# Two small VectorE jobs given to GpSimd in a banded-attention and two-layer MoE kernel, and its instruction order drawn anew

## The chip, the core and the metric

The kernel runs on one core of a Trainium2 chip. Five engines work side by side and wait for each other through semaphores: TensorE (PE: matmuls and transposes, with PEld its weight loads), VectorE (DVE), ScalarE (ACT), GpSimd (POOL) and SyncE (SP), whose queue issues all the DMAs here. The metric is the device time of one execution in microseconds (us). It is compared as the median over several runs.

## The reference, cut to what matters

```python
out_d = softmax(scale * mean4(q) @ mean4(k).T) @ mean4(v)     # "global": groups of 4 positions
out_local = softmax(mask(|i - j| < 4, scale * q @ k.T)) @ v   # "local": a band
x = repeat4(out_d) + out_local                                # 2304 tokens x 512
h = x @ w_in                                                  # 512 -> 1024
ln = layernorm(h * softmax(h)) * g_ln
x = ln @ w_out                                                # 1024 -> 512
h = x @ w2_in                                                 # 512 -> 2048
out = (h * cos(h)) @ w2_out                                   # 2048 -> 512
```

Four batches of 8 heads, 576 positions and 64 columns a head; 2304 tokens in the two layers. The weights and activations come in as float64 words or float32, and the products must be better than one pass of TensorE's reduced float32 gives.

## The kernel before, in words

**Split products.** Every large matmul is made of three (`mm3`, L506 to L509): a number is split into a high part (`hi`, rounded, fp32r) and a low part (`lo` = number minus `hi`), and hi*hi + hi*lo + lo*hi are summed. `split` (L496 to L504) makes `hi` on ScalarE and `lo` on VectorE, by one subtraction with two inputs in SBUF.

**Weights.** `wload` (L528 to L543) loads a block of a weight as 64-bit words and makes float32 of it in three VectorE operations: a shift and mask (L537), an or with the sign (L539), an or with the low word's bits (L541). The first weight, `w1i`, comes in 8 blocks of 512 KB (128 x 512 words); `w1i_step` (L582) loads one and splits it into `w1i_h` and `w1i_l`, two parts of the tile R (in the trace `R<-wu`; in the order's rows `R_75`). `w1o` comes in 8 more.

**Attention.** `Glob.load` (L648) loads the values of one pair of heads as `gv` (72 x 2 x 4 x 128: the four values of a group side by side). `Glob.prep` (L653) sums q and k over groups of four (`pooled`, L661), and the values in two additions: the halves of `gv` (L667, 72 x 512) and then the halves of that into `gvs` (L669, 72 x 256). `Glob.V` multiplies them with the softmax (`gv` in PSUM, L707) into `G`. `Loc.V` makes the local product (`lv`, L770), and one VectorE addition, L772, adds `lv` and `G` into X, the tokens. A 128-token block of X is split (`xsplit`, `P<-X`) and goes into the first layer's matmuls (`h<-R,P`).

**The start.** TensorE has nothing to do until q, k, v and the first weight blocks are there, so 100 matmuls without a use (`idle`, L873) stand in its early gaps. The first `h` needs the first block of X, which needs both pairs of heads of batch 0.

**The order.** `arrange` sorts the instructions of each engine. It replays the whole program with a table of estimated durations (`Step.estimate`), gives each instruction a due time, and shifts the due times of some tiles by a list of seeds, `DRAWS`. The order that comes out is fixed on every engine: an instruction that has to wait holds up what stands behind it on its engine, on SP's queue and on GpSimd too.

Of the kernel before, what the change touches and what calls it, by code (L numbers as in the profile page):

```python
# [9 lines left out]
F32 = mybir.dt.float32  # L10
# [5 lines left out]
ALU = mybir.AluOpType  # L16
# [19 lines left out]
ROUNDS = 20  # L36
SEARCHED = 0.8
DRAWS = (70000001, 70000006, 70000036, 70000042, 70000050, 70000063, 70000081, 70000093, 70000097, 70000106,
# [19 lines left out]

# [73 lines left out]
class Step:  # L132
# [10 lines left out]
    def estimate(self, psum):  # L143
        out, n, kind = self.outs[0], columns(self.outs[0]), self.x.opcode
# [8 lines left out]
        wide = max([n] + [columns(o) for o in self.ins[:1]])  # L153
# [22 lines left out]
        if self.engine == "Pool":  # L176
            return 464 if wide == 1 else 245 + (1.73 if kind == "TensorTensor" else 3.4 if "Ptr" in kind else 0.4) * wide
        return 60.0
# [250 lines left out]
def kernel(  # L429
# [13 lines left out]
    nc = tc.nc  # L443
# [30 lines left out]
    w1i_h = R1[:, 0:W1].rearrange("p (k f) -> p k f", k=KD)  # L474
    w1i_l = R1[:, W1:2 * W1].rearrange("p (k f) -> p k f", k=KD)
# [19 lines left out]

    def split(hi, lo, src, gain=None):  # L496

        if gain is None:
            nc.scalar.activation(out=hi, in_=src, func=AF.Copy)  # L499
            nc.vector.tensor_tensor(out=lo, in0=src, in1=hi.bitcast(F32), op=ALU.subtract)  # L500
        else:
            nc.scalar.activation(out=hi, in_=src, func=AF.Copy, scale=gain)
            nc.vector.scalar_tensor_tensor(out=lo, in0=src, scalar=gain, in1=hi.bitcast(F32),
                                           op0=ALU.mult, op1=ALU.subtract)  # L504
# [22 lines left out]

    def wload(src, place):  # L528

# [4 lines left out]
        low, high = words[:, :, 0], words[:, :, 1]  # L534
        ui = u.bitcast(I32)

        nc.vector.tensor_scalar(out=ui, in0=high, scalar1=3, scalar2=0x3FFFFFFF,  # L537
                                op0=ALU.logical_shift_left, op1=ALU.bitwise_and)
# [43 lines left out]
    def w1i_step(i):  # L582
        k, f = i % KD, slice(i // KD * W1C, (i // KD + 1) * W1C)
        split(w1i_h[:, k, f], w1i_l[:, k, f], wload(w1i[k * 128:(k + 1) * 128, f], stage))

# [39 lines left out]
    class Glob:  # L625
# [27 lines left out]
        def prep(self):  # L653
            if self.a0:
                return
            if self.c % 2 == 0:
                for j in range(2):
# [4 lines left out]
                    if j == 0:  # L662
                        for k in range(2):
                            r = slice(64 * k, 64 * k + 64)
                            nc.scalar.copy(out=pdiag[self.turn][r, :, k], in_=o[r])
            vs = VS[self.b, self.c] = att.tile([SH, 2, 128], F32, tag="gvs", name="gvs", bufs=4)
            nc.vector.tensor_tensor(out=self.v[:, :, 0:2, :], in0=self.v[:, :, 0:2, :], in1=self.v[:, :, 2:4, :],  # L667
                                    op=ALU.add)
            nc.vector.tensor_tensor(out=vs, in0=self.v[:, :, 0, :], in1=self.v[:, :, 1, :], op=ALU.add)  # L669

# [337 lines left out]
    for kk in range(KD):  # L1008
        src = X[:, :TB2, kk, :]
# [237 lines left out]
```

## Time and the profile before

| | before |
|---|---|
| median of 3 runs | 751.3 us (750.54 to 752.64) |
| the profiled execution, its own time | 752.8 us |
| span of its trace, first to last instruction | 751.0 us |
| PE busy | 736.1 us, 98% |
| DVE busy | 607.1 us, 81% |
| ACT busy | 458.3 us, 61% |
| POOL busy | 20.5 us, 3% |
| PE busy with the 100 `idle` matmuls (inside the 736.1) | 17.9 us |

Busy time is the sum of an engine's instruction times within the span. The `idle` matmuls count as busy PE time although they compute nothing that is used. Rows of a timeline give the start, the duration of a merged group, and in brackets how long the engine had been idle before it and what released it.

### The profile page before, as it was taken

Reading aid. Unit: us, or ns where it says so; the run is one execution under the profiler, and the core shown is the slowest. Engines: PE = TensorE matmul, PEld = TensorE weight load, DVE = VectorE, ACT = ScalarE, POOL = GpSimd, SP = SyncE. Lnnn points to the kernel's source line nnn. Section 1 sums busy time; section 2 is a strip of 40 time slices with the busy share of each in tenths; the row PEclk is TensorE's granted clock in tenths of the full one; section 3 lists DMA queues with packets and bytes.
Section 4 is the critical chain, followed back from the end, with each engine's and each line's share of the span. In section 5 each row is a group of like instructions: output and inputs, shape, how many; then the busy total and the mean of one; then the engine's idle time right before and its main releaser. Section 6 shows DMA issues by size and latency. Waiting matters only on the chain.

```text
span 751.0 us, 14309 instructions
## 1 busy us (share of the span) xinstructions
PE 736.1 (98%) x5324; PEld 651.2 (87%) x5324; DVE 607.1 (81%) x1244; ACT 458.3 (61%) x1062; POOL 20.5 (3%) x40
## 2 busy tenths in 40 slices
PE   6899999999999999999999999999999999999998
PEld 5678898898988898889998898899998898898896
DVE  5999999969479799986499996977669676877763
ACT  6477678848465455534577765756556665656654
POOL 3000000000000001000000000000000000000000
PEclk9989999999999999999999999999999999999999
DMA  9956766765265675684354442042212331122201
GB/s 269 278 164 190 214 182 181 192 181 168 69 173 171 213 234 176 206 253 134 99 169 140 127 150 75 29 133 78 79 35 71 113 88 54 29 85 84 60 27 57
DMA packets 76502, 101.92 MB, mean 136 GB/s; under 512 B 23280, under 2 KB 48912, under 8 KB 76432
## 3 DMA queue, kind: packets, MB, share of 16 engines
q1 hardware_dynamic: 76432, 101.00, 44.7%
q8 instruction: 42, 0.69, 0.4%
q14 instruction: 28, 0.23, 0.1%
HBM read 83.67 MB, written 17.30 MB: 134 GB/s over the span
## 4 chain that ended last, share of the span: by engine, by line
PE 73%; DVE 16%; DMA 5%; issue 3%; ACT 2%; SPq 1%; POOL 0%; ACTq 0%; DVEq 0%; POOLq 0%
PE s L507 7%; PE s L508 7%; PE s L509 7%; PE ob L507 4%; PE ob L509 4%; PE ob L508 4%; PE oa L507 4%; PE oa L509 4%; PE oa L508 4%; PE ls L749 3%; PE x L507 3%; PE x L508 3%; PE x L509 3%; PE h L507 3%; PE h L509 3%
## 5 line engine op out<-in xcount | busy, mean ns | idle before, releaser
L508 PE MATMUL x<-P,R 128*128 128x256 f32 x288 | 80.9, 287 | 0.4 <-DVE P L500 0.2
L507 PE MATMUL x<-P,R 128*128 128x256 f32 x288 | 80.5, 288 | 0.3 <-DVE P L500 0.3
L509 PE MATMUL x<-P,R 128*128 128x256 f32 x288 | 80.2, 285 | 0.0
L508 PE MATMUL s<-R 128*128 128x256 f32 x256 | 70.3, 282 | 0.1
L507 PE MATMUL s<-R 128*128 128x256 f32 x256 | 69.9, 283 | 0.5 <-DVE wr L1142 0.2
L509 PE MATMUL s<-R,S_l 128*128 128x256 f32 x256 | 70.1, 282 | 0.0
L507 PE MATMUL h<-R,P 128*128 128x512 f32 x144 | 59.2, 421 | 0.0
L508 PE MATMUL h<-R,P 128*128 128x512 f32 x144 | 57.7, 410 | 0.0
L509 PE MATMUL h<-R,P 128*128 128x512 f32 x144 | 57.4, 409 | 0.0
L508 PEld LDWEIGHTS x<-P,R 128*128 128x128 f32 x288 | 53.5, 188 | 1.9 <-DVE P L500 1.1
L507 PEld LDWEIGHTS x<-P,R 128*128 128x128 f32 x288 | 53.4, 188 | 1.4 <-DVE P L500 0.5
L509 PEld LDWEIGHTS x<-P,R 128*128 128x128 f32 x288 | 53.5, 188 | 0.8 <-issue 0.2
L508 PE MATMUL s<-R,w2i 128*128 128x256 f32 x192 | 52.9, 282 | 0.4 <-DVE R L500 0.4
L507 PE MATMUL s<-R,w2i 128*128 128x256 f32 x192 | 53.0, 281 | 0.0
L509 PE MATMUL s<-R,w2i 128*128 128x256 f32 x192 | 52.7, 281 | 0.0
L609 ACT ACTIVATE le<-ls,sm 128x70 f32<-128x70 f32 x144 | 44.0, 325 | 13.6 <-DVE sm L607 9.7
L1031 ACT ACTIVATE a<-a 128x1024 f32<-128x1024 f32 (+1 forms) x41 | 39.2, 955 | 21.5 <-DVE a L1029 21.1
L499 ACT ACTIVATE GR<-a 128x1024 fp32r<-128x1024 f32 (+1 forms) x41 | 39.3, 958 | 21.0 <-DVE a L1034 20.7
L507 PEld LDWEIGHTS s<-R 128*128 128x128 f32 x256 | 47.4, 188 | 2.1 <-ACT R L499 0.6
L508 PEld LDWEIGHTS s<-R 128*128 128x128 f32 x256 | 47.7, 189 | 1.7 <-DVE R L500 0.7
L509 PEld LDWEIGHTS s<-R,S_l 128*128 128x128 f32 x256 | 47.8, 189 | 0.8
L500 DVE TENSOR_TENSOR GR<-a,GR 128x1024 fp32r<-128x1024 f32 (+1 forms) x41 | 44.7, 1090 | 4.5 <-ACT GR L499 4.2
(171 smaller groups left out, 2167.2 us busy)
## 6 DMA issues: line engine op xcount, KB each, us to landing
wo<-drw SPq DMA_DIRECT2D x80, 256.0 KB
X<-in_w2o_dram SPq DMA_DIRECT2D x32, 256.0 KB
X<-in_w2i_dram SPq DMA_DIRECT2D x32, 256.0 KB
lv<-in_vl_dram SPq DMA_DIRECT2D x48, 105.0 KB
out_dram<-xo SPq DMA_DIRECT2D x18, 256.0 KB
gv<-in_vg_dram SPq DMA_DIRECT2D x16, 256.0 KB
X<-in_w1i_dram SPq DMA_DIRECT2D x8, 512.0 KB
X<-in_w1o_dram SPq DMA_DIRECT2D x8, 512.0 KB
```

Source lines behind the costliest of these rows:

```text
L499: nc.scalar.activation(out=hi, in_=src, func=AF.Copy)
L500: nc.vector.tensor_tensor(out=lo, in0=src, in1=hi.bitcast(F32), op=ALU.subtract)
L507: nc.tensor.matmul(ps, lh, rh, start=start, stop=False)
L508: nc.tensor.matmul(ps, lh, rl, start=False, stop=False)
L509: nc.tensor.matmul(ps, ll, rh, start=False, stop=stop)
L609: nc.scalar.activation(out=e[:, j, :], in_=src[:, j, :], func=AF.Exp, bias=neg[:, j:j + 1], scale=scale, accum_out=ssum[:, j:j + 1])
L749: nc.tensor.matmul(ps[:, i:i + WIN], self.q[:, h, a].rearrange("p j s -> p (j s)"), self.k[:, h, a * QB:a * QB + WIN], start=False, stop=h ...
L1031: nc.scalar.activation(out=a, in_=a, func=AF.Sin, scale=0.5)
```

## The change

`split` and `wload` get an argument `on`, the engine that does one of their operations. `w1i_step` passes GpSimd to `split`: the 8 low parts of the first weight (128 x 512 each) are subtracted by GpSimd. No caller passes `on` to `wload`, so nothing changes there. `Glob.prep` lets GpSimd make both additions of the values for batches 0 and 1, which are 8 pairs of additions (8 of 72 x 512 and 8 of 72 x 256), and leaves batches 2 and 3 on VectorE. The planner's figure for a GpSimd operation with two inputs goes from 1.73 to 2.2 a column. `DRAWS` is another list, of 202 seeds where there were 201, and `SEARCHED` goes from 0.8 to 1, so that shifts can lie anywhere in the program. Line numbers after the list move by 1 or 2.

```diff
-SEARCHED = 0.8
-DRAWS = (70000001, 70000006, 70000036, 70000042, 70000050, 70000063, 70000081, 70000093, 70000097, 70000106,
...
+SEARCHED = 1
+DRAWS = (10000004, 10000024, 10000025, 10000029, 10000044, 10000050, 10000051, 10000058, 10000071, 10000081,
...
-            return 464 if wide == 1 else 245 + (1.73 if kind == "TensorTensor" else 3.4 if "Ptr" in kind else 0.4) * wide
+            return 464 if wide == 1 else 245 + (2.2 if kind == "TensorTensor" else 3.4 if "Ptr" in kind else 0.4) * wide
...
-    def split(hi, lo, src, gain=None):
+    def split(hi, lo, src, gain=None, on=nc.vector):
...
             nc.scalar.activation(out=hi, in_=src, func=AF.Copy)
-            nc.vector.tensor_tensor(out=lo, in0=src, in1=hi.bitcast(F32), op=ALU.subtract)
+            on.tensor_tensor(out=lo, in0=src, in1=hi.bitcast(F32), op=ALU.subtract)
...
-        split(w1i_h[:, k, f], w1i_l[:, k, f], wload(w1i[k * 128:(k + 1) * 128, f], stage))
+        split(w1i_h[:, k, f], w1i_l[:, k, f], wload(w1i[k * 128:(k + 1) * 128, f], stage), on=nc.gpsimd)
...
-            nc.vector.tensor_tensor(out=self.v[:, :, 0:2, :], in0=self.v[:, :, 0:2, :], in1=self.v[:, :, 2:4, :],
+            on = nc.gpsimd if self.b < 2 else nc.vector
+            on.tensor_tensor(out=self.v[:, :, 0:2, :], in0=self.v[:, :, 0:2, :], in1=self.v[:, :, 2:4, :],
                                     op=ALU.add)
-            nc.vector.tensor_tensor(out=vs, in0=self.v[:, :, 0, :], in1=self.v[:, :, 1, :], op=ALU.add)
+            on.tensor_tensor(out=vs, in0=self.v[:, :, 0, :], in1=self.v[:, :, 1, :], op=ALU.add)
```

The order on VectorE, around the addition that completes the first block of X. Before, it stands 72nd, behind the last two value sums (L667, L669) and the fourth low part of the weight (L500):

```order
L661 TENSOR_REDUCE pooled_113<-qt 128x288
L667 TENSOR_TENSOR gv<-gv 72x2x256 x2
L669 TENSOR_TENSOR gvs<-gv 72x256 x2
L500 TENSOR_TENSOR R_75<-wu,R_75 128x512
L537 TENSOR_SCALAR wu<-X 128x512 x2
L539 SCALAR_TENSOR_TENSOR wu<-X,wu 128x512
L772 TENSOR_TENSOR X<-lv,g 128x3x128
L541 SCALAR_TENSOR_TENSOR wu<-X,wu 128x512
```

The same place now; the addition is L774:

```order
L614 TENSOR_TENSOR ge<-ge,sm 96x288
L608 TENSOR_SCALAR sm<-sm 96x2 x2
L662 TENSOR_REDUCE pooled_113<-qt 128x288
L538 TENSOR_SCALAR wu<-X 128x512
L540 SCALAR_TENSOR_TENSOR wu<-X,wu 128x512
L542 SCALAR_TENSOR_TENSOR wu<-X,wu 128x512
L774 TENSOR_TENSOR X<-lv,g 128x3x128
L538 TENSOR_SCALAR wu<-X 128x512
```

Ahead of that addition VectorE has lost 4 additions of 72 x 512, 4 of 72 x 256, 4 subtractions of 128 x 512 and one shift of 128 x 512, and has gained one or (L542) of 128 x 512; every other instruction ahead of it is the same in kind and number, in another order.

GpSimd now has these rows directly behind its memsets and masks at the start. Before, the next row there was the `pow` of the first layer norm (L827):

```order
L669 TENSOR_TENSOR gv<-gv 72x2x256
L671 TENSOR_TENSOR gvs<-gv 72x256
L669 TENSOR_TENSOR gv<-gv 72x2x256
L671 TENSOR_TENSOR gvs<-gv 72x256
L501 TENSOR_TENSOR R_75<-wu,R_75 128x512 x2
L669 TENSOR_TENSOR gv<-gv 72x2x256
L501 TENSOR_TENSOR R_75<-wu,R_75 128x512
L671 TENSOR_TENSOR gvs<-gv 72x256
L501 TENSOR_TENSOR R_75<-wu,R_75 128x512
L669 TENSOR_TENSOR gv<-gv 72x2x256
L671 TENSOR_TENSOR gvs<-gv 72x256
L501 TENSOR_TENSOR R_75<-wu,R_75 128x512 x4
```

The last of the four `gvs` of batch 0, which the first X needs, stands behind four low parts of the weight.

On TensorE, ahead of the first `h` (`h_645` is the bank of the first half). Before, the last `idle` stands in front of 8 `gv`, 12 `lv` and 6 transposes:

```order
L873 MATMUL idle<-mask,identb 128x350
L707 MATMUL gv<-at,gvs 64x48 x8
L770 MATMUL lv<-at,lv 64x64 x12
L689 MATMUL gt<-ident,ge 72x96 x6
L507 MATMUL h_645<-R_75,P 128x512
```

Now those `lv` and half of those `gv` stand earlier, and `idle` matmuls stand behind the last 4 `gv` too:

```order
L709 MATMUL gv<-at,gvs 64x48 x4
L875 LDWEIGHTS identb
L875 MATMUL idle<-mask,identb 128x350
L875 LDWEIGHTS identb
L875 MATMUL idle<-mask,identb 128x350
L875 LDWEIGHTS identb
L875 MATMUL idle<-mask,identb 128x350
L691 MATMUL gt<-ident,ge 72x96 x6
L508 MATMUL h_645<-R_75,P 128x512
L509 MATMUL h_645<-R_75,P 128x512
```

All 100 `idle` still stand ahead of the first `h`. SP's queue has the third and fourth `gv` load (256 and 32 KB each) behind three and four of the `w1i` blocks; before, all four stood ahead of the first block.

## Rows read from the trace of the kernel before

**Rows 1.** The page, part 1: busy time, share of the span, instructions.
```profile
span 751.0 us, 14309 instructions
PE 736.1 (98%) x5324; PEld 651.2 (87%) x5324; DVE 607.1 (81%) x1244; ACT 458.3 (61%) x1062; POOL 20.5 (3%) x40
```

**Rows 2.** Stretch; busy us (instructions) of PE, PEld, DVE, ACT, POOL; clock, DMA share, GB/s.
```profile
0.00:40.00 40.00, 31.27 (x260) 23.33 (x261) 31.45 (x80) 22.22 (x79) 6.88 (x22) 0.97 0.89 263
...
60.00:140.00 80.00, 79.81 (x704) 69.01 (x702) 79.97 (x204) 60.57 (x220) 3.33 (x5) 1.00 0.66 188
140.00:350.00 210.00, 208.68 (x1724) 187.87 (x1724) 176.31 (x501) 119.12 (x372) 10.31 (x13) 1.00 0.60 182
350.00:740.00 390.00, 389.05 (x2459) 349.24 (x2459) 299.99 (x414) 239.06 (x326) 0.00 (x0) 1.00 0.28 85
```

**Rows 3.** Timeline of TensorE up to the first `h`.
```profile
29.78 4.17 PE L873 MATMUL idle<-mask,identb 128*128 128x350 bf16 x27
35.72 0.68 PE L707 MATMUL gv<-at,gvs 72*64 72x48 f32 x16 [1.77 <-DVE gvs L669]
...
38.31 0.85 PE L689 MATMUL gt<-ident,ge 96*72 96x96 f32 x4 [0.90 <-DVE X L772]
38.97 0.80 PE L507 MATMUL h<-R,P 128*128 128x512 f32 x1
```

**Rows 4.** Timeline of VectorE: its first instruction, and the same stretch.
```profile
6.44 1.35 DVE L661 TENSOR_REDUCE pooled<-qt 128x288 f32<-128x1152 f32 x1 [6.44 <-DMA qt<-in_q_dram]
...
33.96 1.28 DVE L667 TENSOR_TENSOR gv<-gv 72x512 f32<-72x512 f32 x2
35.16 0.75 DVE L669 TENSOR_TENSOR gvs<-gv 72x256 f32<-72x256 f32 x2
35.83 0.68 DVE L500 TENSOR_TENSOR R<-wu,R 128x512 fp32r<-128x512 f32 x1
36.43 0.75 DVE L537 TENSOR_SCALAR wu<-X 128x512 int32<-128x512 int32 x2
37.10 0.68 DVE L539 SCALAR_TENSOR_TENSOR wu<-X,wu 128x512 int32<-128x512 int32 x1
37.71 0.55 DVE L772 TENSOR_TENSOR X<-lv,g 128x384 f32<-128x384 f32 x1
38.17 0.68 DVE L541 SCALAR_TENSOR_TENSOR wu<-X,wu 128x512 int32<-128x512 int32 x1
38.77 1.34 DVE L661 TENSOR_REDUCE pooled<-kt 128x288 f32<-128x1152 f32 x1
```

**Rows 5.** Groups of GpSimd by shape: columns as in part 5 of a page.
```profile
L827 POOL TENSOR_TENSOR st<-st,nhalf 128x1 f32<-128x1 f32 x18 | 13.6, 758 | 322.3 <-DVE st L825 303.4 <-DVE R L500 18.8
L868 POOL TENSOR_SCALAR_AFFINE_SELECT mask<-mask 64x350 bf16<-64x350 bf16 x4 | 2.0, 498 | 0.2
...
L868 POOL TENSOR_SCALAR_AFFINE_SELECT mask<-mask 64x70 bf16<-64x70 bf16 x4 | 1.0, 240 | 0.1
```

**Rows 6.** Instructions of two lines: duration ns min/median/max, first and last start.
```profile
L827 POOL TENSOR_TENSOR st<-st,nhalf x18: 548/604/1341, 71.3 to 343.3; 128x1 f32<-128x1 f32 x18
...
L500 DVE TENSOR_TENSOR w2i<-X,w2i x16: 413/416/422, 268.0 to 312.4; 128x256 fp32r<-128x256 f32 x16
```

**Rows 7.** Timelines of GpSimd and VectorE around one `pow`.
```profile
268.27 1.14 POOL L827 TENSOR_TENSOR st<-st,nhalf 128x1 f32<-128x1 f32 x1 [1.27 <-DVE st L825]
...
268.05 0.42 DVE L500 TENSOR_TENSOR w2i<-X,w2i 128x256 fp32r<-128x256 f32 x1
268.38 0.42 DVE L539 SCALAR_TENSOR_TENSOR X<-X 128x256 int32<-128x256 int32 x1
```

**Rows 8.** The chain that ended last, about 9 us: start, length, what.
```profile
9.06 3.77 DMA lv<-in_vl_dram
```

**Rows 9.** Busy time by stretch, columns as in group 2.
```profile
35.00:40.00 5.00, 3.38 (x50) 2.81 (x51) 5.00 (x10) 2.27 (x7) 0.00 (x0) 0.76 0.74 202
40.00:45.00 5.00, 5.00 (x21) 4.14 (x21) 4.35 (x11) 2.85 (x12) 0.00 (x0) 0.56 0.52 156
```

More of the change, by code (lines that the diff above doesn't have):

```diff
@@ L494 @@
     xh1, xl1 = [part((2 * KF + i * KD) * GT, 2, KD, 128) for i in range(2)]
-    def split(hi, lo, src, gain=None):
+    def split(hi, lo, src, gain=None, on=nc.vector):
         if gain is None:
             nc.scalar.activation(out=hi, in_=src, func=AF.Copy)
-            nc.vector.tensor_tensor(out=lo, in0=src, in1=hi.bitcast(F32), op=ALU.subtract)
+            on.tensor_tensor(out=lo, in0=src, in1=hi.bitcast(F32), op=ALU.subtract)
         else:
             nc.scalar.activation(out=hi, in_=src, func=AF.Copy, scale=gain)
-            nc.vector.scalar_tensor_tensor(out=lo, in0=src, scalar=gain, in1=hi.bitcast(F32),
+            on.scalar_tensor_tensor(out=lo, in0=src, scalar=gain, in1=hi.bitcast(F32),
                                            op0=ALU.mult, op1=ALU.subtract)
@@ L525, in bank, with wload @@
         return psum.tile([128, 512], F32, tag=tag, name=name, bufs=bufs)
-    def wload(src, place):
+    def wload(src, place, on=nc.vector):
         n = src.shape[1]
@@ L535, in wload @@
         ui = u.bitcast(I32)
-        nc.vector.tensor_scalar(out=ui, in0=high, scalar1=3, scalar2=0x3FFFFFFF,
+        on.tensor_scalar(out=ui, in0=high, scalar1=3, scalar2=0x3FFFFFFF,
                                 op0=ALU.logical_shift_left, op1=ALU.bitwise_and)
```

39 rows, old and new, of the table DRAWS are left out of this document.

## The prediction

> **What bounds the kernel now.** I read the page first: PE is busy for 736.1 of 751.0 us, with POOL almost unused [rows 1]. A share over the whole run hides where the rest lies, so the second view is busy time by stretch. From 60 to 140 us PE is busy for 79.81 of 80, from 140 to 350 for 208.68 of 210, from 350 to 740 for 389.05 of 390 [rows 2]: over 680 us it lacks 0.19 + 1.32 + 0.95 = 2.46 us. There TensorE is the bound. VectorE is busy too, 79.97 of 80 us between 60 and 140, but TensorE does not wait for it, so time taken off VectorE there buys at most those tenths. What can be won lies in the first 40 us: PE is busy for 31.27 of them, and 17.9 us of that are the useless `idle` matmuls (the table above). Afterwards the useful matmuls run as a queue that is always full, so the end of the run moves by as much as its start moves.
>
> The third view is TensorE's timeline up to that start. The `idle` run out at 33.95, PE waits 1.77 us for the value sum L669 and 0.90 us for the addition L772, and the first `h` starts at 38.97 [rows 3]. The fourth is VectorE's timeline in the same stretch: its instructions stand back to back, two L667, two L669, a low part L500, then L772 at 37.71 [rows 4]; ScalarE makes the high part behind it, and `h` follows. So the first `h` comes when VectorE has worked through what stands ahead of L772.
>
> **What is taken from VectorE ahead of L772.** I use the distance from one start to the next, since neighbours overlap by some 0.08 us [rows 4]: L667 twice takes 35.16 - 33.96 = 1.20, so 0.60; L669 twice 35.83 - 35.16 = 0.67, so 0.335; L500 36.43 - 35.83 = 0.60; L537 twice 37.10 - 36.43 = 0.67, so 0.335; L541 38.77 - 38.17 = 0.60. The order takes away 4 L667, 4 L669, 4 L500 and one L537 and puts in one L541: 2.40 + 1.34 + 2.40 + 0.335 - 0.60 = 5.9 us. All other rows ahead of it are the same, so without a new wait the first `h` starts at 38.97 - 5.9 = 33.1. The other operations that leave VectorE (4 low parts, 4 pairs of sums of batch 1) stand behind the first `h`, where TensorE is the bound; I cost them at nothing. Their cover is the queue of ready matmuls in 60 to 140 us, where VectorE would even have to fall back to cost anything.
>
> **What GpSimd gets.** Ahead of that X it has 12 operations in a row: 4 sums of 72 x 512, 4 of 72 x 256 and 4 low parts of 128 x 512. The trace shows none of this kind. The nearest rows have one input: 0.240 us for 70 columns, 0.498 for 350 [rows 5], so 0.92 ns a column, and 512 columns at least 0.65 us. If each of two inputs costs that much, 512 columns take 0.24 + 2 x 0.92 x 442 = 1.05 us and 256 columns 0.58 us, an estimate; I take it, as the only price that counts both inputs. The 12 are then 8 x 1.05 + 4 x 0.58 = 10.7 us (6.8 by one input: 8 x 0.65 and 4 x 0.41). The Trainium skill (GPSIMD Engine Reference, Performance versus the Vector engine) gives 4497 ns for a two-input addition of 2048 columns, 1.12 us for 512; by that the 12 would be about 11.2 us. No run here shows it yet.
>
> When can they start? The queue issues a `lv` load at 9.06, just behind the four `gv` loads, and it lands 3.77 us later [rows 8], so the `gv` are there by about 12.8. The third and fourth `gv` now stand behind up to four blocks of 512 KB: 4 x 0.524 MB at 263 GB/s [rows 2] are 8 us, so the fourth lands near 21, and its two sums end near 23; the 12 in a row, from 12.8 on, near 23.5. The last `gvs` is needed 3.1 us ahead of the first `h` (35.91 against 38.97 now [rows 3, 4]), so by 30.0 where `h` comes at 33.1. GpSimd has over 6 us in hand there, and its slower arithmetic costs nothing by itself.
>
> **What the two engines do to each other.** This is the unknown. The 18 `pow` of 128 x 1 take 548 ns at least but 1341 at most [rows 6] and 758 on the mean [rows 5]. At 268.27 one takes 1.14 us while VectorE runs an L500 and an L539 one behind the other [rows 7]: GpSimd is held up by VectorE. The other way nothing is seen: that L500 keeps to 0.42 us, and the 16 of its shape lie between 413 and 422 ns [rows 6]. But a `pow` reads one column, and the new operations read 512. Bounds: VectorE loses nothing, or it stands still for all 10.7 us. I take the mean hold-up of the `pow`, 758 - 548 = 0.21 us, for each of the 12: 2.5 us. It is near the lower bound because the nearest rows show no stretched VectorE instruction at all.
>
> The Trainium skill (SBUF — State Buffer, Who interferes with whom) speaks against the change: a VectorE instruction with two SBUF inputs and a GpSimd one that reads SBUF exclude each other, and the later one waits for the whole of the earlier. The stretched `pow` agrees with one half of that; the other half is not in this trace. By this rule the sum would be that of the second rival below.
>
> **The sum.** The first `h` moves by 5.9 - 2.5 = 3.4 us, to 35.6. The profiled execution would take 752.8 - 3.4 = 749.4 us; it lay 1.5 above the median of the runs, so the median goes from 751.3 to **747.9 us**. A difference under 0.3% (2.25 us) is about what a measurement of this kernel cannot tell from none.
>
> **The rest of the new order** moves thousands of rows. The instructions on TensorE are the same in number, and of the stretches behind 60 us only 2.46 us can be won; a new order can lose that much as easily. I cost it at nothing, with about 1.5 us either way.
>
> **Rivals.**
>
> *The clock stays up.* Behind the gaps at 34 to 38 us the granted clock is 0.76 of 2.4 GHz in 35 to 40 and 0.56 in 40 to 45 [rows 9], which is time at the 1.2 GHz level; it costs 5 x 0.24 + 5 x 0.44 = 3.4 us of full-speed work. In the new order three `idle` stand between the last `gv` and the transposes ahead of `h`, so the gaps may be filled. If the clock does not fall: 747.9 - 3.4 = 744.5. Against it: a GpSimd that is late opens the same gaps.
>
> *VectorE is held.* A GpSimd operation that has begun holds any VectorE instruction with two SBUF inputs. VectorE's list ahead of L774 takes 37.71 - 6.44 - 5.9 = 25.4 us [rows 4], and over 6 us of it are such instructions (10 ors of 0.60, and 8 smaller products of the softmax). If half of GpSimd's 10.7 us falls on them, VectorE loses 5.4, and 0.5 of the 5.9 is left: 750.8. For it: the hold-up is seen in one direction. Against it: most of the list can run meanwhile.
>
> *GpSimd is late (slower).* Its 12 operations stand in one queue, and the first X waits for the last of them. They end near 23.5 without waits and cost nothing until 35.9, so this decides from (35.9 - 23.5)/12 = 1.0 us of waiting per operation. At 1.5 us each, about twice the longest wait of a `pow` (0.79), the last `gvs` comes at 41.5, 5.6 us later than now: 756.9. VectorE's back-to-back ors are what could starve it.
>
> *The move does nothing*, because the loads set the pace: the DMA share is 0.89 over the first 40 us [rows 2]. Then 751.3. VectorE is busy in all of 35 to 40 [rows 9], which speaks against it.
>
> **Chances.** My forecast (746 to 750) 0.40; the clock stays up (744.5) 0.19; VectorE held (750.8) 0.23; GpSimd late (756.9) 0.13; nothing 0.05. Of the forecast's 0.40 a small part lies above 749.05, and some of "held" lies below it: faster by over 0.3% 0.60, within 0.3% 0.26, slower 0.14. The range for 8 in 10 reaches from 743.0, under the clock's case, to 753.0, over that of a held VectorE and short of a late GpSimd.
>
> **What would show it.** The first `h` near 35.6 us and not 38.97; 12 GpSimd operations ahead of the last `gvs`, of about 1.05 and 0.58 us plus waits; VectorE's two-input instructions (0.68 us for 512 columns) no longer than now; PE with no more than 3 us of gaps behind 60 us. It is wrong if those VectorE instructions stretch to a microsecond or more beside GpSimd, if PE waits for POOL ahead of the first `gv`, or if the first `h` moves and the end does not.

## The result, and the profile after

| | before | changed |
|---|---|---|
| median | 752.0 us (750.5 to 752.7, 4 runs) | 762.0 us (760.9 to 763.6, 4 runs) |
| ratio, with its 95% interval | 1 | 1.0138 (1.0113 to 1.0162) |
| profiled execution, its span | 752.8, 751.0 us | 763.6, 761.5 us |
| first `h` | 38.97 us | 42.83 us |

The change makes the kernel slower, by 10 us. The page of the changed kernel, part 1, against [rows 1]:

```profile
span 761.5 us, 14324 instructions
...
PE 741.1 (97%) x5324; PEld 652.8 (86%) x5324; DVE 607.1 (80%) x1220; ACT 457.3 (60%) x1062; POOL 55.9 (7%) x64
```

VectorE has lost 24 instructions and is busy for exactly as long as before, 607.1 us. So those that are left have become longer by as much as was saved. The timeline of VectorE in the changed kernel, ahead of the addition L774 that completes the first X (start, length, and in brackets an idle time):

```profile
12.68 0.31 DVE L612 TENSOR_SCALAR sm<-sm 128x6 f32<-128x6 f32 x1 [1.97 <-ACT le L610]
...
13.25 1.55 DVE L614 TENSOR_TENSOR le<-le,sm 128x420 f32<-128x420 f32 x1
...
24.85 1.64 DVE L542 SCALAR_TENSOR_TENSOR wu<-X,wu 128x512 int32<-128x512 int32 x1
...
28.05 1.16 DVE L608 TENSOR_SCALAR sm<-sm 96x2 f32<-96x2 f32 x1
29.14 0.68 DVE L542 SCALAR_TENSOR_TENSOR wu<-X,wu 128x512 int32<-128x512 int32 x1
...
30.16 2.16 DVE L614 TENSOR_TENSOR ge<-ge,sm 96x144 f32<-96x144 f32 x1
...
36.12 1.31 DVE L608 TENSOR_SCALAR sm<-sm 96x2 f32<-96x2 f32 x2
37.35 1.34 DVE L662 TENSOR_REDUCE pooled<-qt 128x288 f32<-128x1152 f32 x1
...
39.14 1.10 DVE L540 SCALAR_TENSOR_TENSOR wu<-X,wu 128x512 int32<-128x512 int32 x1
40.28 0.69 DVE L542 SCALAR_TENSOR_TENSOR wu<-X,wu 128x512 int32<-128x512 int32 x1
40.89 0.55 DVE L774 TENSOR_TENSOR X<-lv,g 128x384 f32<-128x384 f32 x1
```

The L542 at 24.85 takes 1.64 us, the one at 29.14 takes 0.68, as its kind did before [rows 4]. Seven rows ahead of L774 are more than 0.2 us longer than their kind in the trace of before, by 6.8 us together. And here is GpSimd in the same stretch:

```profile
10.90 1.26 POOL L669 TENSOR_TENSOR gv<-gv 72x512 f32<-72x512 f32 x1 [2.76 <-DMA gv<-in_vg_dram]
12.24 0.72 POOL L671 TENSOR_TENSOR gvs<-gv 72x256 f32<-72x256 f32 x1
...
24.20 1.74 POOL L501 TENSOR_TENSOR R<-wu,R 128x512 fp32r<-128x512 f32 x1 [8.82 <-ACT R L500]
27.23 1.97 POOL L501 TENSOR_TENSOR R<-wu,R 128x512 fp32r<-128x512 f32 x1 [1.29 <-ACT R L500]
29.16 1.78 POOL L669 TENSOR_TENSOR gv<-gv 72x512 f32<-72x512 f32 x1
30.90 1.26 POOL L501 TENSOR_TENSOR R<-wu,R 128x512 fp32r<-128x512 f32 x1
...
36.14 1.27 POOL L501 TENSOR_TENSOR R<-wu,R 128x512 fp32r<-128x512 f32 x1 [2.89 <-ACT R L500]
37.37 1.45 POOL L669 TENSOR_TENSOR gv<-gv 72x512 f32<-72x512 f32 x1
38.90 0.80 POOL L671 TENSOR_TENSOR gvs<-gv 72x256 f32<-72x256 f32 x1
```

Lay the two views on each other: each stretched VectorE row begins while a GpSimd operation runs, or within 0.02 us of its start, and ends with it or within 0.6 us behind it, as if it had waited and then run. The longest, at 30.16, outlasts two operations, the L669 of 29.16 and the L501 of 30.90. The L542 of 24.85 ends at 26.49, 0.55 behind the L501 of 24.20 to 25.94; the L608 at 28.05, of two columns, ends at 29.21 with the L501 that ends at 29.20. The reduction at 37.35 runs beside an L669 and keeps its 1.34 us. GpSimd in turn waits three times for ScalarE's high parts (L500), which wait for VectorE's ors, so its last sum of batch 0 ends at 39.70 and not near 23.5.

X needs that sum as well as VectorE. Behind the sum come the last 8 `gv` on TensorE and `g` on ScalarE:

```profile
38.50 1.66 PE L875 MATMUL idle<-mask,identb 128*128 128x350 bf16 x10
40.09 0.44 PE L709 MATMUL gv<-at,gvs 72*64 72x48 f32 x8
```

```profile
35.44 0.63 ACT L500 ACTIVATE R<-wu 128x512 fp32r<-128x512 f32 x1 [1.09 <-DVE wu L542]
40.57 0.25 ACT L712 ACTIVATE g<-gv 128x96 f32<-128x96 f32 x1 [0.98 <-PE gv L709]
```

`g` is ready at 40.82, just as VectorE comes to the end of its L542 and X starts at 40.89. Both paths end together, and both go back to the stretched rows: GpSimd's low part at 36.14 waits for ScalarE's R of 35.44, which waits for a VectorE or that ends at 35.40, and 5.3 of the 6.8 us of stretch lie ahead of that.

Behind the first `h`, the row of TensorE's timeline with its longest wait there, and the windows around it against [rows 2, 9] (busy us of PE, PEld, DVE, ACT, POOL; clock, DMA share, GB/s):

```profile
60.78 0.85 PE L761 MATMUL lt<-ident,le 128*70 128x128 f32 x3 [1.79 <-DVE X L774]
```

```profile
55.00:60.00 5.00, 3.99 (x41) 2.89 (x41) 5.00 (x7) 3.75 (x14) 4.84 (x5) 1.00 0.97 334
60.00:65.00 5.00, 4.22 (x36) 3.30 (x37) 4.69 (x14) 2.44 (x7) 0.92 (x1) 0.57 0.32 107
65.00:70.00 5.00, 5.00 (x25) 4.81 (x25) 3.25 (x11) 2.78 (x13) 0.00 (x0) 0.50 0.16 37
70.00:75.00 5.00, 5.00 (x20) 4.14 (x20) 3.87 (x8) 3.73 (x12) 0.00 (x0) 0.57 0.47 143
```

From 55 to 60 us VectorE is busy all the time with 7 instructions, GpSimd with 5; TensorE runs dry and waits for the next X, and behind that gap the granted clock is at the 1.2 GHz level for most of 60 to 75. That costs 5 x (0.43 + 0.50 + 0.43) = 6.8 us of full-speed work, against 3.4 before [rows 9]. In this one execution the 10.5 us between the spans are thus: 3.9 from the later first `h`; 4.0 more in gaps of TensorE behind it (10.2 against 6.2 us); and 2.6 by which TensorE's busy time behind the first `h` is longer (708.5 against 705.9 us for the same work), which is the longer matmuls of the low clock (less than the 3.4 between the two sums above, since part of the low clock falls on gaps, and in before a part lies ahead of `h`). Of the 4.0 us of gaps 2.3 lie ahead of 80 us and 1.8 behind it. From 140 to 350 us, for instance, TensorE is now busy for 207.18 us, where it was 208.68 [rows 2]:

```profile
140.00:350.00 210.00, 207.18 (x1701) 184.54 (x1700) 179.92 (x514) 120.63 (x389) 14.50 (x13) 1.00 0.62 188
```

### The profile page after: what moved, and what is told of

Its sections match the earlier page's. It is cut to its first block, busy times and chain, and to the rows that moved or that the text cites. A ratio compares the mean times of both kernels' runs of the same rounds, so it can differ in the third digit from the quotient of the medians.

```text
span 761.5 us, 14324 instructions
## 1 busy us (share of the span) xinstructions
PE 741.1 (97%) x5324; PEld 652.8 (86%) x5324; DVE 607.1 (80%) x1220; ACT 457.3 (60%) x1062; POOL 55.9 (7%) x64
## 4 chain that ended last, share of the span: by engine, by line
PE 71%; DVE 19%; ACT 4%; issue 3%; DMA 3%; POOL 1%; DVEq 0%; POOLq 0%; ACTq 0%; SPq 0%
PE s L508 6%; PE s L509 6%; PE s L510 6%; PE ob L510 4%; PE oa L508 4%; PE oa L510 4%; PE oa L509 4%; PE ob L508 4%; PE ob L509 4%; PE ls L751 3%; PE x L509 3%; PE x L508 3%; PE x L510 3%; PE h L508 2%; PE h L510 2%
## 5 line engine op out<-in xcount | busy, mean ns | idle before, releaser
L509 PE MATMUL x<-P,R 128*128 128x256 f32 x288 | 78.7, 287 | 2.0 <-DVE P L501 2.0
L508 PE MATMUL x<-P,R 128*128 128x256 f32 x288 | 78.4, 287 | 0.0
L510 PE MATMUL x<-P,R 128*128 128x256 f32 x288 | 77.9, 284 | 0.0
L508 PE MATMUL h<-R,P 128*128 128x512 f32 x144 | 60.5, 425 | 0.7 <-ACT P L500 0.7
L509 PE MATMUL h<-R,P 128*128 128x512 f32 x144 | 59.0, 415 | 0.0
L510 PE MATMUL h<-R,P 128*128 128x512 f32 x144 | 57.8, 409 | 0.3 <-DVE P L501 0.3
L509 PEld LDWEIGHTS x<-P,R 128*128 128x128 f32 x288 | 52.6, 188 | 3.2 <-DVE P L501 2.9
L500 ACT ACTIVATE GR<-a 128x1024 fp32r<-128x1024 f32 (+1 forms) x41 | 39.2, 958 | 25.8 <-DVE a L1036 22.3
L508 PEld LDWEIGHTS x<-P,R 128*128 128x128 f32 x288 | 52.5, 188 | 0.8 <-ACT P L500 0.4
L510 PEld LDWEIGHTS x<-P,R 128*128 128x128 f32 x288 | 52.6, 188 | 0.1
L500 ACT ACTIVATE w2i<-wo 128x512 fp32r<-128x512 f32 x58 | 36.0, 624 | 24.8 <-PE ob L510 14.3
```

The costliest lines, as they stand in the source:

```text
L508: nc.tensor.matmul(ps, lh, rh, start=start, stop=False)
L509: nc.tensor.matmul(ps, lh, rl, start=False, stop=False)
L510: nc.tensor.matmul(ps, ll, rh, start=False, stop=stop)
```

## The experiments

Three theories. **HOLD**: a GpSimd operation that reads SBUF stops VectorE's instructions. **LATE**: GpSimd is slower and waits for ScalarE, and TensorE waits for its results. **ORDER**: the new order is a worse one, whoever makes the sums. The times of all kernels, with the first `h` and the stretch (how much longer VectorE's rows ahead of the first X are than in before, rows by more than 0.2 us) of the profiled execution, and TensorE's gaps in it (its idle time from 80 to 740 us):

| kernel | median us | ratio to before, 95% | first `h` | stretch | gaps |
|---|---|---|---|---|---|
| before | 752.0 | 1 | 38.97 | 0 | 2.45 |
| changed | 762.0 | 1.0138 (1.0113 to 1.0162) | 42.83 | 6.8 | 4.25 |
| x1 new order, sums on VectorE | 756.2 | 1.0059 (1.0039 to 1.0079) | 39.99 | 0 | 4.82 |
| x2 old order, sums on GpSimd | 756.0 | 1.0050 (1.0031 to 1.0068) | 41.99 | 6.4 | 2.30 |
| x3 old order, weight only | 755.1 | 1.0044 (1.0025 to 1.0063) | 41.69 | 2.6 | 2.11 |
| x4 old order, values only | 753.2 | 1.0031 (1.0019 to 1.0044) | 40.78 | 4.3 | 1.92 |
| x6 old order, first pair only | 751.7 | 1.0010 (0.9997 to 1.0023) | 39.27 | 1.1 | 2.47 |
| x7 changed, memsets | 750.6 | 0.9993 (0.9980 to 1.0006) | 40.32 | 2 (below) | 4.03 |
| x8 changed, copies | 751.7 | 1.0009 (0.9994 to 1.0023) | 38.60 | 1.6 | 5.39 |
| x11 changed, two copies each | 756.5 | 1.0069 (1.0053 to 1.0085) | 39.93 | 2.6 | 6.31 |
| x9 before, no seeds | 758.9 | 1.0106 (1.0091 to 1.0121) | 39.05 | 0 | 5.93 |
| x10 changed, no seeds | 770.2 | 1.0258 (1.0218 to 1.0297) | 42.17 | 6.3 | 3.61 |

The five kernels with the new order (changed, x1, x7, x8, x11) have 4.0 to 6.3 us of gaps, the five with the order of before 1.9 to 2.5, whichever engine makes the sums (one trace of each). That is a cost of the new order of its own, 1.5 us or more.

### The two engines by themselves (m1_port)

```diff
+    for i in range(16):
+        V.tensor_tensor(out=c, in0=a, in1=b_, op=ALU.add)
+        if i < 10:
+            G.tensor_tensor(out=f, in0=d, in1=e, op=ALU.add)
...
```

> This kernel leaves the whole computation out and times the two engines against each other, stage by stage: VectorE alone, GpSimd alone, and both, with five kinds of VectorE instruction beside GpSimd additions of 128 x 512, and one stage with GpSimd memsets. Theory HOLD (a GpSimd operation that reads SBUF holds VectorE instructions with two SBUF inputs or in the two-column mode): beside GpSimd additions of about 1.27 us, VectorE additions of 512 columns go from 0.68 us alone to 1.5 us or more where one falls behind a GpSimd operation, and so do tensor_scalar instructions, even of 6 columns; reductions and additions with one input in PSUM keep their 0.6 to 0.7 us; beside memsets the additions keep 0.68 us. Theory ORDER or LATE (VectorE is not held, the time is lost by the new order or by waiting for GpSimd): VectorE durations are the same in all stages within 5%.

Its groups by shape (count | busy us, mean ns); the alone case of each engine comes first, then VectorE beside GpSimd's additions (beside its memsets in L478):

```profile
L467 DVE TENSOR_TENSOR vc<-va,vb 128x512 f32<-128x512 f32 x16 | 11.1, 693 | 0.9 <-ACT vb L461 0.4
L470 POOL TENSOR_TENSOR gc<-ga,gb 128x512 f32<-128x512 f32 x10 | 12.6, 1262 | 17.8 <-ACT vb L461 17.1
L473 DVE TENSOR_TENSOR vc<-va,vb 128x512 f32<-128x512 f32 x16 | 20.5, 1280 | 15.4 <-ACT vb L461 14.9
...
L478 DVE TENSOR_TENSOR vc<-va,vb 128x512 f32<-128x512 f32 x16 | 11.1, 692 | 1.5 <-ACT vb L461 0.9
L483 DVE TENSOR_REDUCE vc<-va 128x1 f32<-128x512 f32 x16 | 11.0, 686 | 1.3 <-ACT va L459 0.8
L488 DVE TENSOR_TENSOR vc<-pp,va 128x512 f32<-128x512 f32 x16 | 11.1, 691 | 3.1 <-ACT va L459 2.6
L493 DVE TENSOR_SCALAR vc<-va 128x512 f32<-128x512 f32 x16 | 16.2, 1015 | 3.1 <-ACT va L459 2.5
L498 DVE TENSOR_SCALAR vc<-va 128x6 f32<-128x6 f32 x32 | 15.0, 467 | 1.8 <-ACT va L459 0.8
L503 DVE TENSOR_TENSOR vc<-va,vb 128x512 f32<-128x512 f32 x12 | 10.5, 879 | 1.3 <-ACT vb L461 0.9
```

An addition of 512 columns takes GpSimd 1.26 us. Beside it (L473) VectorE's additions take 1280 ns instead of 693: 16 x 0.587 / 10 = 0.94 us lost for each GpSimd operation. Beside GpSimd's memsets (L478) the additions lose nothing. As reductions (L483) or with one input in PSUM (L488) VectorE's instructions take 686 and 691 ns; no run has them alone, but GpSimd's additions beside them keep their 1.26 us too, so neither engine seems to lose. Where every other VectorE instruction is a reduction (L503) VectorE's loss is 12 x 0.186 / 10 = 0.22 us, and there GpSimd's additions take 1.60 us instead of 1.26. So an operation of 512 columns that is moved saves VectorE 0.60 us [rows 4] and can cost it 0.94.

The Trainium skill (SBUF — State Buffer, Who interferes with whom) has the same sorting: two SBUF inputs on VectorE against a GpSimd operation that reads, not against one that only writes, and never reductions. The exclusion is not quite whole: ten additions of each engine took 16.7 us, 1.67 a pair, where 1.26 + 0.69 = 1.95 would be one behind the other.

### The order and the move apart (x1, x2, x3)

x1 plans the 24 operations as GpSimd's and then runs them on VectorE; x2 and x3 plan them as VectorE's, in the order of before, and then run 24 or 8 of them on GpSimd. The other three engines keep their order.

```diff
+    kept[dve] = sorted(kept[dve] + [i for i in kept[pool] if steps[i].moved], key=lambda i: start[i])
+    kept[pool] = [i for i in kept[pool] if not steps[i].moved]
```

> The new order on all engines, but the 24 operations run on VectorE, at the places where the plan had them start. HOLD: about 752 to 755 us, since the stretched VectorE instructions (7 us of excess ahead of the first X) are gone and 5.9 us of plain work come back there. ORDER: 760 to 763, as the changed kernel. LATE: below 752, since no GpSimd is waited for and the order is a newer one.

> The old order on all engines, but the 24 operations run on GpSimd, in the order in which they stood on VectorE. HOLD: 756 to 763 us, with VectorE instructions of over 1 us beside the GpSimd ones. ORDER: 747 to 752, since the bad order is not there and VectorE has less to do. LATE: 753 to 757 with unchanged VectorE durations and TensorE waiting for GpSimd.

> The old order, with the 8 low parts of the first weight alone on GpSimd. HOLD: slower than before by 2 to 6 us, in proportion to 8 of 24 operations and 10.2 of about 26 us of GpSimd time (1.27 us each), most of them beside the two-input ors of the next weight block. ORDER: 749 to 752. LATE: within 1 us of the old kernel, as the low parts are needed late.

Each half alone costs 4.5 to 4.7 us, both together 10.0: ORDER and the move share the loss. Read the other way, the same 24 operations on GpSimd take 756.0 us in the old order and 762.0 in the new one. x1 lies above what HOLD gave for it (752 to 755) and below ORDER's 760; x2 lies at the lower end of HOLD's range and inside LATE's; x3, with 2.6 us of stretch, inside HOLD's alone. In x1 nothing is stretched and the clock stays up; TensorE waits later, for ScalarE at 73.56 (1.22 us) and for VectorE at 320.93 (1.46). In x2 VectorE's rows stretch by 6.4 us, and TensorE waits for GpSimd as well:

```profile
36.75 0.44 PE L714 MATMUL gv<-at,gvs 72*64 72x48 f32 x8 [1.84 <-POOL gvs L676]
37.89 0.51 PE L714 MATMUL gv<-at,gvs 72*64 72x48 f32 x8 [0.70 <-POOL gvs L676]
```

That is 2.5 us, but TensorE waits 1.77 us for the same sums in before [rows 3], so LATE adds 0.8. In the changed kernel `idle` matmuls stand in that place and no such wait shows, though the sum comes late there too.

### Parts of the move (x4, x6)

```diff
+            on = nc.gpsimd if self.b == 0 and self.c < 2 else nc.vector
+            on.tensor_tensor(out=self.v[:, :, 0:2, :], in0=self.v[:, :, 0:2, :], in1=self.v[:, :, 2:4, :],
+                                    op=ALU.add)
+            on.tensor_tensor(out=vs, in0=self.v[:, :, 0, :], in1=self.v[:, :, 1, :], op=ALU.add)
```

(x6; x4 has `self.b < 2`.)

> The order of before on every engine, with only the 16 sums of the values of batches 0 and 1 on GpSimd and the low parts of the weight left on VectorE. Ahead of the first X, VectorE loses 8 instructions (4 x 0.60 + 4 x 0.335 = 3.7 us). Before takes 751.5 in the same call. HOLD (a GpSimd operation that reads SBUF and VectorE instructions stop each other, about 0.6 us lost per GpSimd operation): 8 operations take back about 4.8 us, the first h comes at 39 to 41, the time is 752 to 754, and VectorE shows two or more instructions above 1 us ahead of the first h that took 0.6 before. LATE (the slower engine alone: PE waits for the last gvs from GpSimd): VectorE's instructions keep their lengths, PE's wait ahead of the last gv rows grows, 752 to 755. NEITHER (the sums are a good thing to move, the weight's low parts are the bad one): first h at 35 to 37, 748 to 750.

> The order of before, with only the four sums of the first pair of heads (2 of 72 x 512, 2 of 72 x 256) on GpSimd, which come at about 11 to 16 us, where VectorE is at reductions for half of the time; the reductions were not stretched when the two engines ran alone. VectorE loses 2 x 0.60 + 2 x 0.335 = 1.9 us ahead of the first X. If few of VectorE's instructions meet GpSimd's there (only the 128 x 420 product and two of 96 x 144), the first h comes 1 to 1.9 us earlier, at 37 to 38, and the time is 749.5 to 750.5, a version better than both. HOLD at the average price of 0.6 us per GpSimd operation: 2.4 us taken back, first h at 39 to 39.5, 751.5 to 752.3. LATE: no, the sums are needed only at 30 us.

x4 came at 753.2, in the ranges of HOLD and of LATE; its 4.3 us of stretch and its first `h` at 40.78 are HOLD's. x6 was the attempt at a version that beats both kernels, and is level with before. VectorE's timeline in x6:

```profile
14.90 0.58 DVE L612 TENSOR_REDUCE sm<-ls 128x6 f32<-128x420 f32 x1
...
15.52 1.24 DVE L613 TENSOR_SCALAR sm<-sm 128x6 f32<-128x6 f32 x1
```

The reduction at 14.90 keeps its time; the `tensor_scalar` of six columns behind it starts 50 ns after a GpSimd addition (15.47 to 16.72), takes 1.24 us instead of 0.17, and eats 1.1 of the 1.9 us. VectorE's idle time ahead of the first X is 0.85 us longer too, so X comes at 38.01 (before 37.71).

### The same order, with less read by GpSimd (x7, x8, x11)

The changed kernel, instruction for instruction in its order on the other engines and on VectorE; only what the 24 GpSimd operations do is changed (x8 shown; x7 has memsets; x11 the second copy as well). In x7 and x8 they are shorter too, and the low parts of the weight don't wait for ScalarE's high parts; x11 gives both back:

```diff
-            on.tensor_tensor(out=lo, in0=src, in1=hi.bitcast(F32), op=ALU.subtract)
+            nc.gpsimd.tensor_copy(out=lo, in_=src)
...
+            nc.gpsimd.tensor_copy(out=lo, in_=hi.bitcast(F32))
```

> The changed kernel with its own order on every engine, but each of GpSimd's 24 operations is a memset of the same output, so GpSimd reads no SBUF there (this leaves the low parts of the first weight and the sums of the values of batches 0 and 1 out of the computation). A memset of 512 columns takes 0.52 us instead of 1.26 and does not wait for ScalarE's high part. HOLD: the 7 us by which VectorE's instructions were stretched ahead of the first X vanish, X comes at about 34 instead of 40.89, first h at 35 to 37, and the time falls from 762 by 6 to 9, to 753 to 756, where what is left over 751.5 is the new order's. ORDER (the loss sits in the new order alone, and GpSimd only shares in it): the time stays within 2 of 762. A stretched VectorE row beside a memset would speak against HOLD.

> The changed kernel with its own order on every engine, but each of GpSimd's 24 operations is a copy of one of its two inputs, so GpSimd reads one operand from SBUF instead of two (this leaves the subtractions of the first weight's low parts and the sums of the values of batches 0 and 1 out of the computation). It tells what about the operation does the holding. If any GpSimd read of SBUF holds VectorE as an addition does: VectorE's rows ahead of the first X still stretch by 4 us or more in all, first h at 39 to 42, 758 to 762. If only operations with two inputs hold it, the run looks like the one with memsets, first h at 35 to 37, 753 to 756. If the hold goes with the time that GpSimd reads: a one-input copy of 512 columns takes 0.6 to 0.8 us by the one-input rows of before, about half of 1.26, so half of the 7 us, 757 to 759.

> The changed kernel with its own order, but each of GpSimd's 24 operations is two copies in a row, one of each of its two inputs, to the same output (this leaves the subtractions of the low parts of the first weight and the sums of the values of batches 0 and 1 out of the computation). So GpSimd takes as long as with additions (2 x 0.61 = 1.22 us against 1.26), reads the same bytes, and waits for ScalarE's high part as it did there; only two inputs at once are gone. LATE (GpSimd's length and its wait for the high part carry the loss, and the kernels with memsets and single copies were fast because theirs were shorter): first h at 41 to 43, 759 to 762. HOLD BY TWO INPUTS: VectorE's rows ahead of the first X stretch by 1 to 3 us in all instead of 6.8, first h at 38.5 to 40, 750.5 to 753. In between, 754 to 758, both carry it.

x7 and x8 take back the whole loss, more than expected. So in this order what GpSimd's operations do carries the loss: the order alone doesn't make a slow kernel. That does not make the order free. Both kernels have taken 24 operations off VectorE and are only level with before, and each gains something else: the clock never falls in them, while before loses 3.4 us there. x8's first `h` is 0.4 us earlier than before's and TensorE's busy time behind it 3.8 us shorter (702.0 against 705.9), but its gaps behind the first `h` are 3.0 us longer (9.2 against 6.2). x7's first `h`, expected at 35 to 37, is at 40.32, 1.35 us later than before's, and its end is level. The old order with copies was not run, so how the 10 us divide between the move and the order is not settled. (That x1 loses because its order has no room for 24 more operations on VectorE is possible; no run shows it.)

What stands ahead of X in x8:

```profile
34.28 1.66 PE L895 MATMUL idle<-mask,identb 128*128 128x350 bf16 x10
35.87 0.44 PE L729 MATMUL gv<-at,gvs 72*64 72x48 f32 x8
```

```profile
36.64 0.56 DVE L794 TENSOR_TENSOR X<-lv,g 128x384 f32<-128x384 f32 x1 [0.87 <-ACT g L732]
```

GpSimd's last `gvs` is done at 33.10, but TensorE's fixed order has 10 `idle` matmuls ahead of the last 8 `gv`, 1.6 us of work that nobody uses; TensorE goes through them and on to the `gv` without a pause, and ScalarE's `g` and X wait for that. The new order pays here with its own `idle`.

The window of x8 around the place of the changed kernel's gap:

```profile
60.00:80.00 20.00, 20.00 (x161) 16.07 (x159) 20.00 (x51) 14.70 (x55) 4.60 (x5) 1.00 0.55 157
```

In 60 to 80 TensorE is busy for all 20 us at the full clock; the changed kernel has 19.22 us and a clock of 0.66 there.

x7 speaks against one part of HOLD as I had put it. VectorE and, behind it, the last four of six memsets in a row that GpSimd begins at 26.73, in x7:

```profile
26.79 2.13 DVE L624 TENSOR_SCALAR sm<-sm 96x2 f32<-96x2 f32 x1
26.85 2.07 DVE L558 SCALAR_TENSOR_TENSOR wu<-X,wu 128x512 int32<-128x512 int32 x1
```

```profile
27.45 1.93 POOL L515 MEMSET R<- 128x512 f32 x4
```

A `tensor_scalar` of two columns takes 2.13 us beside memsets, which read nothing; the three rows behind it begin meanwhile, at their usual distances, and all end at the same 28.92, so the loss is some 1.1 us, and which of the four rows was held can't be read from it. With one of 0.95 at 22.08 that is about 2.

x11 lies where the expectation had put both theories: GpSimd takes as long as in the changed kernel (a copy takes 0.61 us alone, two 1.22) and waits for ScalarE as there. By the ratios 0.6% of the 1.3% between x8 and the changed kernel are lost again, 4.5 of 9.7 us; the other 5.2 need two inputs in one operation. Ahead of the first `h`, where x11 is 1.3 us behind x8, the trace tells what it is: TensorE waits 0.33 and 0.64 us for GpSimd's sums, and VectorE stands idle for 1.54 us at X until `g` is there, so that is LATE. How the rest of the 4.5, behind the first `h`, divides between length and held instructions (copies hold too, see below), x11 does not tell.

### One input or none, by themselves (m2_one_input)

```diff
-            G.tensor_tensor(out=f, in0=d, in1=e, op=ALU.add)
+            G.tensor_copy(out=f, in_=d)
...
+            G.memset(f, 2.0)
```

> VectorE and GpSimd by themselves again, the whole computation left out; now GpSimd's operations have one input or none. Alone, a tensor_scalar of 512 columns and one of 6 set the base. From the kernel whose GpSimd copies instead of adding: the addition of VectorE beside GpSimd copies should lose much less than the 0.94 us per GpSimd operation that it lost beside additions. PORT BY TWO INPUTS: 0 to 0.2 us lost per copy. ANY READ HOLDS: a copy takes 0.61 us, and the loss is 0.4 us or more per copy. From the kernel with memsets, where a tensor_scalar of 96 x 2 took 2.13 us and one of 128 x 512 1.36 beside rows of memsets: a tensor_scalar should be held beside memsets, by 0.2 us or more per memset, although an addition was not (692 ns with and without). If it isn't, those rows in the kernel waited for something else.

Groups by shape: `tensor_scalar` of 512 and of 6 columns alone (L467, L470), an addition, and both `tensor_scalar` beside ten copies (L473, L478, L483), both beside ten memsets (L488, L493):

```profile
L467 DVE TENSOR_SCALAR vc<-va 128x512 f32<-128x512 f32 x16 | 6.8, 427 | 0.7 <-ACT va L459 0.2
L470 DVE TENSOR_SCALAR vc<-va 128x6 f32<-128x6 f32 x32 | 5.5, 172 | 1.8 <-ACT va L459 0.7
L473 DVE TENSOR_TENSOR vc<-va,vb 128x512 f32<-128x512 f32 x16 | 14.0, 872 | 1.4 <-ACT vb L461 0.9
L478 DVE TENSOR_SCALAR vc<-va 128x512 f32<-128x512 f32 x16 | 9.7, 608 | 1.3 <-ACT va L459 0.8
L483 DVE TENSOR_SCALAR vc<-va 128x6 f32<-128x6 f32 x32 | 8.5, 265 | 1.8 <-ACT va L459 0.8
L488 DVE TENSOR_SCALAR vc<-va 128x512 f32<-128x512 f32 x16 | 9.6, 602 | 1.3 <-ACT va L459 0.8
L493 DVE TENSOR_SCALAR vc<-va 128x6 f32<-128x6 f32 x32 | 9.3, 292 | 1.8 <-ACT va L459 0.8
```

With these bases the first run's `tensor_scalar` rows can be read: beside additions they lost 16 x (1.015 - 0.427) / 10 = 0.94 us, and those of six columns 32 x (0.467 - 0.172) / 10 = 0.94, per GpSimd operation. The same price as for VectorE's additions, whatever VectorE's instruction takes itself. A copy costs 0.29 us of VectorE's time (0.29, 0.29 and 0.30 in the three cases), a memset 0.28 or 0.38 where VectorE does a `tensor_scalar` and nothing where it adds. So neither of the two expectations on copies was right: they hold VectorE, by a third of an addition's price. That makes the memsets the likely cause of the stretched rows in x7.

### Without the lists of seeds (x9, x10)

```diff
-DRAWS = (10000004, 10000024, 10000025, 10000029, 10000044, 10000050, 10000051, 10000058, 10000071, 10000081,
...
+DRAWS = ()
```

> The kernel before with an empty list of seeds: the planner's order without any shifts. It is the base for the next run. A list chosen from many must be worth something: 752 to 765.

> The changed kernel with an empty list of seeds: the move to GpSimd under the planner's own order, beside the kernel before without seeds. HOLD (the cost belongs to two-input operations on GpSimd, whatever the order): 4 us or more above the kernel before without seeds, with stretched VectorE rows ahead of the first h. LIST (the new list of seeds is a bad one and carries the loss): within 3 us of the kernel before without seeds, and not above the changed kernel's 762.

Without its list the kernel before takes 758.9 us and the changed one 770.2: the move, with the order that the planner makes for it, costs 11.3 us without lists, as it costs 10 with them, and there are 6.3 us of stretched rows ahead of the first X. In the profiled executions 9.8 us lie between the spans, 3.1 of them at the first `h` and 6.8 in TensorE's longer busy time behind it (715.2 against 708.4 us): here the late X is paid for mostly in clock. Each list is worth 8 to 9 us to its own kernel, so LIST falls: the new list does as much for its kernel as the old one does.

## Why the prediction was wrong, step by step

**What bounds the kernel** was read rightly in one half: the loss comes out of the first 80 us, 8.7 of the 10.5 us. But that "the end of the run moves by as much as its start moves" is wrong. The changed kernel's first `h` moves by 3.9 and its end by 10.5; x7's first `h` is 1.35 us late and its end level. Gaps and clock behind the first `h` weigh more than the start. That VectorE alone sets the first X holds for before; in the changed kernel GpSimd's last sum comes to the same time, and in x7, x8 and x11 X waits for `g` with VectorE idle.

**The step that failed is the price of the hold-up**, 0.21 us for each of the 12 operations, 2.5 us. It measured 6.8 us, 0.57 for each; back to back it is 0.94 for 512 columns. The prediction's own first sign of being wrong, VectorE instructions of a microsecond or more beside GpSimd, is what came. The 0.21 came from a `pow` that reads one column, and it was put near the lower bound because the rows of before show no stretched VectorE instruction [rows 6]. They show that a `pow` does not hold VectorE: the L539 of [rows 7] begins 0.11 us inside one and keeps its 0.42 us. That says nothing of an operation that reads 512 columns, and the prediction carried it over. The upper bound (10.7 us for 12 operations, 0.89 each) was near what two loaded engines give. The second rival, VectorE held for half of GpSimd's time, named the mechanism and took 5.4 us for it. It counted only two-input products and ors as exposed; the short `tensor_scalar`s of the softmax are too, and one that begins beside a GpSimd operation can wait out nearly all of it (the L608 at 28.05: 1.16 us instead of 0.15).

**The 5.9 us taken from VectorE** are right as a count, and buy little even where nothing holds. In x8, with 1.6 us of stretch, X is at 36.64, 1.1 us earlier than before, and the first `h` at 38.60, 0.4 earlier: VectorE is idle for 2.9 us more ahead of X, 0.9 of it at the X addition itself, which waits for `g` and so for the 10 `idle` matmuls quoted above; and TensorE waits 0.73 us for ScalarE's `P`, since in the new order a weight block's R stands ahead of `P` on ScalarE. The changed kernel's VectorE is idle for 2.0 us more than before (4.1 against 2.1; the 1.97 in the first row quoted above is the longest wait), and its TensorE has the same 0.73. So **"the rest of the new order costs nothing"**, put at 1.5 us either way, failed as well: ahead of the first `h` by these waits, and behind 80 us by 1.8 us more gaps. The account of the changed kernel: 6.8 of stretch, 2.0 of idle, less 5.9 saved and 0.3 of an earlier start, are 2.6 of the 3.2 us by which X is late (0.6 is not accounted for); and 0.7 more from X to `h`, which gives the 3.9. Against the forecast first `h`, 35.6, that is 7.2 us, of which the hold-up, 6.8 and not 2.5, makes 4.3.

**GpSimd's work**: 1.26 us alone for 512 columns and 0.72 for 256, not the estimated 1.05 and 0.58; beside VectorE 1.48, 1.45 and 0.94 on the mean. That they would end near 23.5 was wrong because I looked only at when the loads come. The low parts need ScalarE's high parts, those need VectorE's ors, and the value sums stand behind them in one queue. "GpSimd is late" was the rival that ended slower, and its rule fits: the last `gvs` at 39.70, and the 3.1 us that the prediction has from there to `h`, give 42.8. It had GpSimd starved by VectorE's ors at 1.5 us for each operation, though; here GpSimd waits three times, 13.0 us in all, for ScalarE's high parts, which come only when VectorE's ors are done. By itself LATE is seen in x11.

**Behind the first `h` nothing was costed**, with VectorE's cover given as a queue of ready matmuls from 60 us on. This is 6.6 of the 10.5 us. GpSimd holds VectorE in 42 to 60 us too, before that queue is filled: five rows there are 3.7 us longer than their kind, three of them right ahead of the X of 60.18. The gap of 1.79 us at 60.78 follows, and the half clock. The clock's rival had the sign reversed in the profiled execution, 6.8 us lost instead of none. It is not the whole of the difference: two of the four timed executions had a mean clock of 0.998 and 0.997 and still took 761.8 and 760.9 us, against 763.6 and 762.2 at 0.990. What those two lost instead stays open, since no trace of them was taken.

## What to carry to other kernels

Before an operation moves from VectorE to GpSimd, list what VectorE runs beside it. If those are instructions with two SBUF inputs or `tensor_scalar`s, even of two columns, then a two-input operation of 512 columns saves VectorE 0.60 us and takes up to 0.94 from it: it can be a loss where VectorE is the bound, which is just where one wants to move things. Reductions and instructions with one input in PSUM run on undisturbed here, and copies cost a third; and a stage must also be searched for the waits that come next (here `idle` matmuls ahead of a useful one in TensorE's fixed order, and the place of `P` on ScalarE), since the time that is freed goes there first.

## What the runs showed that I had not expected

The loss per GpSimd addition is 0.94 us for VectorE's additions of 0.69 us, its `tensor_scalar`s of 0.43 and those of 0.17 alike: it is set by GpSimd's operation. A memset, which reads nothing, takes 0.28 to 0.38 us from `tensor_scalar`s and nothing from additions. And two kernels with a first `h` 0.4 us earlier and 1.35 us later than before end level with it and with each other (751.7 and 750.6 us): the clock never fell in them, and more gaps of TensorE, in the second also the later start, took back what that gave.
